# A new instruction order for a one-core linear-attention and feed-forward kernel, with other loads, buffers and step sizes

## The chip, the core and the metric

The kernel runs on one core of a Trainium2 chip. The core has a matrix engine (TensorE, PE in the profile), three engines for elementwise work (VectorE or DVE, ScalarE or ACT, GpSimd or POOL) and a queue engine (SyncE or SP). They run side by side, each its own instructions in the order of the program, and wait for one another by semaphores. DMA transfers are issued from POOL or from SP. The metric is the time of one execution on the device, in microseconds, median of several runs.

## The reference

Two stages follow each other. The first is a linear recurrence over 768 steps, for 4 batches and 8 heads of 48 channels, with a state of 48x48 for each head:

```python
for t in range(S):
    cur = np.einsum('bhd,bhe->bhde', u[None] * kt, vt)
    y[:, :, t] = np.einsum('bhd,bhde->bhe', rt, state + cur)
    state = wt[:, :, :, None] * state + np.einsum('bhd,bhe->bhde', kt, vt)
```

The second takes y as 3072 rows of 384 numbers (8 heads by 48) and computes

```python
a = x @ w1            # 384 -> 1024
b = x @ w2            # 384 -> 1024
h = a * b @ w3        # 1024 -> 1024
return h @ w_out      # 1024 -> 384
```

Inputs and output are float32.

## The kernel before

**Chunks and units.** The 768 steps are cut into 6 chunks of 128. A unit is one chunk of one or two batches: `UNITS` lists 13 of them, units 0 and 1 with one batch each, the others with two. A chunk's work is done with matrix products: the decay of a step inside the chunk is a cumulative sum of log(w), which `cs` (and, for some units, its transpose `csT`) gets from a product with a triangular matrix `LT`.

**Steps of a unit.** Each is a named step, recorded by `@op` and issued later. Loads: `win`, `kin`, `rin`, `vin`. ACT: `ln` (logarithm of w), then exponentials of the sums: `pc` (the chunk's decay), `ne`, and, by kind of unit, `iw` and `e`, or `et`. DVE: `KRk` and `KRr` (k and r scaled by decays), `rk`, `ruk`, `dg`, `dv` (the term with u). PE: `trk` and `trr` (transposes; `trke` and `trre` copy them out), `m` (the 128x128 products of r and k), `y` (with the state and with the masked `m`), `kv` (the new state's part), `yt` (transposes of y). DVE or ACT: `msk` (mask and copy `m`; or `mcp` on ACT and `maff` on DVE or POOL for the pairs in `POOL_MASK`), `T`, `S`, `Sb` (the state), `yb`, `xT`. In the sets `DMA_R`, `DMA_K` and `DMA_Y` a unit's transposes go by DMA from SP instead (`dtr`, `dtk`, `dty`). Units in `RAW` transpose r itself and multiply by `et`.

**Feed-forward.** w3 and w_out are multiplied first, into `w34` (`wt`: 4 transposes of 128x128 each, `w3Te` copies them out, `wm` 8 products, `w34e` copies out). Then for each unit, in pieces of 512 PSUM columns, `a` and `b` (6 products of 256 columns for a unit with two batches, 12 of 128 else), `asb` copies `a` out (ACT), `abT` multiplies the two (DVE). `o` is 8 products of 384 columns for 128 rows, `osb` copies out, `st` stores from SP.

**Order.** A long list, `ORDER`, names each step with its engine in the order in which it is issued; each engine runs its own steps of the list in that order. `BANKS` names the PSUM bank of each step. `warm` steps are products of zeros without a use of their own. Loads from POOL carry 8 semaphores in turn, so that the ninth waits until the first has landed.

**Lines.** In the profile L323 is any unit load, L350 a w3 load, L334 and L338 w1 and w2, L403 `ln`, L415 and L420 `cs`, L360 `wt`, L364 `w3Te`, L369 `wm`, L573 `m`, L592 `msk`, L608 and L614 `y`, L668 `kv`, L713 `a` and `b`, L724 `abT`, L730 `o`, L737 `osb`, L495, L510 and L642 the DMA transposes, L304 `warm`, L231 `table`. The step `table` asks for one set of ScalarE functions that holds both logarithm and exponential, and it is the first step on ACT.

Of the kernel before, what the change touches and what calls it, by code (L numbers as in the profile page):

```python
# [57 lines left out]
KRr_0@DVE m_1_0@PE mask@POOL KRk_0@DVE warm5@2 trk_0@PE rk_0@DVE kin_2@POOL msk_1_0@DVE trke_0@ACT warm5@2 m_0_0@PE
w3_2@POOL msk_0_0@DVE w1_0@POOL warm5@5 wm_1@PE w2_0@POOL wm_0@PE w1_1@POOL w3Te_3@ACT w34e_1@DVE y_0@PE w3Te_2@ACT
w34e_0@DVE y_1@PE win_3@POOL kv_0@PE kv_1@PE S_0@DVE wm_3@PE ln_2@ACT S_1@DVE Sb_1@DVE Sb_0@ACT w2_1@POOL csT_2@PE  # L60
w34e_3@ACT ruk_0@DVE vin_2@POOL wm_2@PE ruk_1@DVE et_2@ACT dg_0@DVE dg_1@DVE dv_0@DVE rin_3@POOL cs_2@PE w34e_2@DVE
trr_2@PE pc_2@ACT rk_2@DVE yd_0@PE ne_2@ACT dv_1@POOL KRr_2@DVE yb_0@ACT yt_0@PE yd_1@PE KRk_2@DVE w3_3@POOL wt_6_0@PE
wt_4_0@PE wt_7_0@PE xT_0@DVE wt_5_0@PE yb_1@DVE trk_2@PE ruk_2@DVE yt_1@PE kin_3@POOL a_0_0@PE trke_2@DVE xT_1@ACT
a_1_0@PE dg_2@DVE asb_0_0@ACT m_2_0@PE asb_1_0@ACT win_4@POOL msk_2_0@DVE b_0_0@PE b_1_0@PE abT_0_0@DVE m_2_1@PE
abT_1_0@DVE vin_3@POOL a_0_1@PE msk_2_1@DVE a_1_1@PE asb_0_1@ACT vin_6@POOL ln_3@ACT asb_1_1@ACT cs_3@PE ublk2@POOL
iw_3@ACT kin_5@POOL b_0_1@PE e_3@ACT b_1_1@PE pc_3@ACT ne_3@ACT abT_0_1@DVE kin_4@POOL abT_1_1@DVE kv_2@PE y_2@PE
S_2@DVE Sb_2@DVE rin_4@POOL rw_3@DVE KRr_3@DVE warm1@7 trr_3@PE trre_3@ACT win_5@POOL wt_4_1@PE wt_5_1@PE w3Te_4@ACT
wt_6_1@PE wt_7_1@PE w3Te_5@ACT vin_5@POOL wm_4@PE rk_3@DVE KRk_3@DVE ruk_3@DVE wm_5@PE rin_5@POOL ln_4@ACT w34e_4@DVE
w3Te_6@DVE iw_4@ACT dg_3@DVE cs_4@PE win_8@POOL w3Te_7@ACT wm_6@PE w34e_5@DVE e_4@ACT wm_7@PE vin_4@POOL pc_4@ACT
ne_4@ACT w34e_6@ACT dv_2@POOL kv_3@PE w34e_7@ACT trk_3@PE T_3@DVE o_1_0@PE trke_3@ACT S_3@POOL KRk_4@DVE win_6@POOL  # L70
yd_2@PE o_0_0@PE osb_1_0@DVE yb_2@DVE st_1_0@SP kin_6@POOL m_3_0@PE rk_4@DVE yt_2@PE osb_0_0@DVE rin_7@POOL m_3_1@PE
xT_2@ACT trk_4@PE ruk_4@DVE st_0_0@SP msk_3_1@DVE ln_5@ACT b_2_3@PE win_7@POOL trke_4@ACT a_2_1@PE rw_4@DVE rin_6@POOL
cs_5@PE msk_3_0@DVE iw_5@ACT a_2_2@PE asb_2_1@ACT dv_3@POOL a_2_0@PE e_5@ACT y_3@PE asb_2_2@ACT KRr_4@DVE kin_9@POOL
pc_5@ACT a_2_3@PE ne_5@ACT yb_3@DVE b_2_1@PE asb_2_0@ACT vin_8@POOL KRk_5@DVE trr_4@PE rw_5@DVE yt_3@PE trre_4@ACT
b_2_2@PE Sb_3@DVE xT_3@DVE vin_7@POOL b_2_0@PE KRr_5@DVE abT_2_2@DVE b_3_0@PE kin_7@POOL ln_6@ACT abT_2_0@DVE a_3_2@PE
abT_2_1@DVE asb_2_3@ACT m_4_1@PE a_3_0@PE dg_4@DVE iw_6@ACT win_10@POOL a_3_1@PE asb_3_0@ACT msk_4_1@DVE b_3_3@PE
dv_4@POOL asb_3_1@ACT b_3_2@PE abT_3_0@DVE m_4_0@PE abT_2_3@DVE win_9@POOL a_3_3@PE msk_4_0@DVE ln_7@ACT o_2_1@PE
kin_8@POOL asb_3_2@ACT rk_5@DVE asb_3_3@ACT abT_3_2@DVE y_4@PE iw_7@ACT kin_10@POOL abT_3_3@DVE b_3_1@PE osb_2_1@ACT
rw_7@DVE trr_5@PE st_2_1@SP rin_10@POOL ruk_5@DVE kv_5@PE trre_5@ACT yb_4@DVE kv_4@PE o_2_0@PE rin_8@POOL dg_5@DVE
T_4@DVE yt_4@PE dv_5@POOL osb_2_0@ACT trk_5@PE abT_3_1@DVE st_2_0@SP cs_6@PE xT_4@DVE trke_5@ACT o_3_0@PE rk_6@DVE  # L80
pc_6@ACT ne_6@ACT S_4@POOL T_5@DVE a_4_0@PE e_6@ACT ruk_6@DVE rin_9@POOL a_4_2@PE KRk_6@DVE Sb_4@ACT asb_4_0@ACT
dg_6@DVE a_4_3@PE kin_11@POOL osb_3_0@ACT b_4_1@PE ln_8@ACT rk_7@DVE st_3_0@SP rw_6@DVE win_11@POOL trk_6@PE
asb_4_2@ACT ruk_7@DVE a_4_1@PE iw_8@ACT KRr_6@DVE rin_11@POOL m_5_0@PE trke_6@ACT dv_6@DVE trr_6@PE b_4_0@PE
msk_5_0@DVE asb_4_1@ACT win_12@POOL o_3_1@PE trre_6@ACT abT_4_1@DVE m_6_0@PE abT_4_0@DVE osb_3_1@ACT b_4_2@PE
rin_12@POOL msk_6_0@DVE st_3_1@SP asb_4_3@ACT b_4_3@PE S_5@POOL m_5_1@PE abT_4_2@DVE cs_7@PE mcp_5_1@ACT vin_9@POOL
abT_4_3@DVE m_6_1@PE kv_6@PE dg_7@DVE e_7@ACT o_4_0@PE vin_10@POOL ne_7@ACT maff_5_1@DVE KRr_7@DVE pc_7@ACT
mcp_6_1@ACT y_5@PE KRk_7@DVE o_4_1@PE T_6@DVE osb_4_0@ACT dtr_7@SP vin_11@POOL Sb_5@ACT yb_5@DVE ln_9@ACT kv_7@PE
rk_9@DVE dtk_7@SP osb_4_1@ACT kin_12@POOL yt_5@PE rw_8@DVE iw_9@ACT cs_9@PE xT_5@DVE cs_8@PE st_4_1@SP e_9@ACT
rk_8@DVE b_5_3@PE st_4_0@SP maff_6_1@POOL ne_8@ACT a_5_3@PE pc_9@ACT pc_8@ACT e_8@ACT rw_9@DVE b_5_2@PE dv_7@POOL
T_7@DVE ne_9@ACT y_6@PE ln_10@ACT b_5_0@PE KRr_8@DVE ln_11@ACT a_5_1@PE S_7@POOL yb_6@DVE dtr_8@SP iw_10@ACT a_5_0@PE  # L90
vin_12@POOL ruk_8@DVE asb_5_1@ACT yt_6@PE ruk_9@DVE b_5_1@PE asb_5_0@ACT dg_8@DVE S_6@POOL xT_6@ACT a_5_2@PE
abT_5_0@DVE iw_11@ACT b_6_1@PE dv_8@DVE asb_5_2@ACT a_6_2@PE Sb_6@ACT abT_5_2@DVE b_6_2@PE asb_5_3@ACT abT_5_1@DVE
# [703 lines left out]
```

## Time and profile before

| what | before |
|---|---|
| median of 3 runs | 178.24 us (178.18 to 178.41) |
| span of the profiled execution | 176.7 us |
| around the span (median minus span) | 1.5 us |
| PE, DVE, ACT, POOL busy | 159.3, 131.3, 97.9, 92.8 us |
| mean granted clock of TensorE | 0.997 |
| moved by DMA | 25.70 MB |

The span runs from the first to the last instruction of the execution. A busy share counts an engine's instructions by their own durations; PE's are pipelined, so that its share overstates the work. An engine that is idle while another is full costs nothing; what counts is at which point PE, which carries the last step, was late and by whom.

### The profile page before, as it was taken

The page shows a single profiled execution, that of the slowest core. Times are in us where ns is not written, and L with a number is a line of the kernel's source. Part 1 is how long each engine was busy: PE and PEld are TensorE (multiplying, and loading weights), DVE is VectorE, ACT ScalarE, POOL GpSimd, SP SyncE. Part 2 cuts the span into 40 slices and gives each one's busy share as a digit, 9 for nine tenths or more (in the row PEclk, how much of TensorE's full clock was granted, in tenths as well). Part 3 has the DMA queues.
Part 4 walks back from the last instruction along what each step waited for, and adds up shares of the span by engine and source line. Part 5 has one row for each costly group of instructions (what it writes and reads, how often), then busy time and mean ns, then how long its engine had stood idle before and what let it go on. Part 6 is the DMA issues. An engine that isn't in the chain of part 4 may idle for free.

```text
span 176.7 us, 4637 instructions
## 1 busy us (share of the span) xinstructions
PE 159.3 (90%) x1935; PEld 118.0 (67%) x1935; DVE 131.3 (74%) x209; ACT 97.9 (55%) x160; POOL 92.8 (53%) x91
## 2 busy tenths in 40 slices
PE   2559898979799899999999889899999999999991
...
DVE  6012869857549999999999999987699957944420
...
DMA  5999999999999999999999997352745660151033
GB/s 95 171 164 192 190 195 211 221 177 192 139 169 186 226 192 147 190 170 177 223 193 143 190 120 142 100 125 67 147 108 121 132 153 1 26 156 45 4 113 111
DMA packets 104101, 25.70 MB, mean 145 GB/s; under 512 B 95216, under 2 KB 103024, under 8 KB 104080
## 3 DMA queue, kind: packets, MB, share of 16 engines
...
q14 instruction: 6, 0.05, 0.1%
...
## 4 chain that ended last, share of the span: by engine, by line
PE 67%; DVE 15%; DMA 6%; ACT 5%; issue 3%; SPq 0%; DVEq 0%
PE banks L713 30%; PE banks L730 13%; PE banks L369 6%; DMA win<-in_w_dram 5%; PE banks L573 4%; DVE rk L524 2%; DVE abT L724 2%; PE banks L614 2%; PE banks L415 2%; PE banks L360 2%; DVE rw L482 2%; PE banks L304 2%; DVE Mbf L592 2%; DMA xT<-yb 1%; DVE ruk L544 1%
## 5 line engine op out<-in xcount | busy, mean ns | idle before, releaser
L713 PE MATMUL banks<-xT,w_bf 128*128 128x256 bf16 (+1 forms) x624 | 69.0, 264 | 1.7 <-DVE abT L724 0.8
L713 PEld LDWEIGHTS <-w_bf 128*128 128x128 bf16 x624 | 55.6, 98 | 10.2 <-issue 2.0
L720 ACT COPY a_sb<-banks 128x512 f32<-128x512 f32 x48 | 28.0, 594 | 28.4 <-PE banks L713 20.0
L724 DVE TENSOR_TENSOR abT<-a_sb,banks 128x512 bf16<-128x512 f32 x48 | 31.4, 679 | 11.3 <-PE banks L713 9.1
L730 PE MATMUL banks<-w,abT 128*128 128x384 bf16 x192 | 34.3, 326 | 0.0
L730 PEld LDWEIGHTS <-abT 128*128 128x128 bf16 x192 | 18.2, 98 | 10.7
L592 DVE TENSOR_TENSOR Mbf<-banks,mask 128x1024 bf16<-128x1024 f32 x16 | 19.5, 1216 | 3.7 <-PE banks L573 3.7
L559 POOL TENSOR_TENSOR dv<-vin,dg 128x768 bf16<-128x768 bf16 (+1 forms) x10 | 14.9, 1497 | 8.6 <-issue 5.5
L323 POOL DMA_DIRECT2D vin<-in_v_dram x13 | 14.6, 1123 | 5.6 <-issue 3.9
L323 POOL DMA_DIRECT2D win<-in_w_dram x11 | 12.9, 1176 | 6.6 <-issue 4.1
L323 POOL DMA_DIRECT2D kin<-in_k_dram x13 | 14.6, 1126 | 1.7 <-DMA w_bf<-in_moe_w_dram 1.0
L737 ACT COPY osb<-banks 128x384 f32<-128x384 f32 x16 | 7.8, 486 | 13.8 <-PE banks L730 13.8
L323 POOL DMA_DIRECT2D rin<-in_r_dram x13 | 14.5, 1119 | 0.6 <-DMA vin<-in_v_dram 0.3
L304 PE MATMUL banks<-zeros 128*128 128x512 bf16 x29 | 9.8, 461 | 3.4 <-DVE zeros L235 3.4
L403 ACT ACTIVATE lw<-win 128x768 bf16<-128x768 f32 (+1 forms) x13 | 10.4, 811 | 4.5 <-DMA win<-in_w_dram 4.5
L369 PE MATMUL banks<-wo_bf,w3T 128*128 128x384 bf16 x64 | 11.2, 326 | 1.1 <-ACT w3T L364 1.1
L587 POOL TENSOR_SCALAR_AFFINE_SELECT Mbf<-Mbf 128x1024 bf16<-128x1024 bf16 x4 | 4.8, 1188 | 14.3 <-ACT Mbf L579 14.3
L550 DVE TENSOR_REDUCE dg<-ruk 128x16 f32<-128x768 bf16 (+1 forms) x13 | 11.4, 879 | 0.0
L573 PE MATMUL banks<-KRT 64*128 64x128 bf16 x192 | 9.6, 218 | 1.0 <-ACT Mbf L579 0.5
L415 PE MATMUL banks<-lw,LT 128*128 128x384 bf16 x24 | 6.4, 341 | 4.3 <-ACT lw L403 4.3
L364 ACT COPY w3T<-banks 128x1024 bf16<-128x1024 bf16 x6 | 6.0, 1016 | 7.3 <-PE banks L360 3.7
L633 DVE TENSOR_TENSOR yb<-banks,dv 128x768 bf16<-128x768 f32 x10 | 9.5, 952 | 0.7 <-PE banks L614 0.4
...
## 6 DMA issues: line engine op xcount, KB each, us to landing
...
```

The source lines that it names most:

```text
L304: nc.tensor.matmul(banks[:, at, :], lhsT=zeros[:, :C], rhs=zeros, start=True, stop=True)
L323: QUEUE[eng].dma_start(dst, src)
L369: nc.tensor.matmul(one(f"wm{fi}")[:, :DM], lhsT=w3T[fi % 2][:, gi, :], rhs=wo_bf[:, gi, :], start=(gi == 0), stop=(gi == FI - 1))
L403: nc.scalar.activation(LW[:, :, :D], ww, Act.Ln)
L550: nc.vector.reduce_sum(dgs, ruks, axis=AX.X)
L559: e.tensor_mul(dvs, vv, dgs[:, :, None].to_broadcast([C, bh, D]))
L573: nc.tensor.matmul(o[:, e, q, :], lhsT=KRTs[a:a + PAD, 0, b * HP + q, :], rhs=KRTs[a:a + PAD, 1, b * HP + q, :], start=True, stop=True)
L592: nc.vector.tensor_mul(Mbf[m], mview(), mask.rearrange("s (j q) t -> s j q t", j=2))
L713: nc.tensor.matmul(o[:, f, :], lhsT=wt[:, di, fi * P:(fi + 1) * P], rhs=x[:, di, :T], start=(di == 0), stop=(di == DI - 1))
L720: copier(eng)(sa, one(f"a{t}_{g}"))
L724: nc.vector.tensor_mul(ab[:, g * per:(g + 1) * per, :T], sa.rearrange("p (f t) -> p f t", t=T), one(f"b{t}_{g}").rearrange("p (f t) -> p f ...
L730: nc.tensor.matmul(one(f"o{t}_{b}")[:, :DM], lhsT=ab[:, fi, b * C:(b + 1) * C], rhs=w34[:, fi, :], start=(fi == 0), stop=(fi == FI - 1))
```

## The change

All 13 units compute the same as before. What changes:

- `ORDER` and `BANKS` are new as a whole. In the new order the transposes for `w34`, and `a` and `b`, come after more of the attention of units 0 to 3; `a` and `b` of units 0 to 3 are issued mixed; `o` comes later behind its `abT`.
- Buffers: `abT` has 8 instead of 3, `xT` 4 instead of 3. Buffers of `Mbf`, `a_sb` and `osb` are named in `BANKS` instead of taken in turn.
- Loads: r, k and v of unit 0 come by SP as float32 and are cast on chip (`rc` and `vc` on ACT, `kc` on DVE); u comes by SP as float32 and is cast by `uc` on DVE. w of units 0 and 1 came by SP before and still does. `ucol`, `ublk` and `ublk2`, whose result nothing read, are gone. w3's four loads are cut by rows (two blocks of 128 rows, all columns) instead of by quarters (four blocks, half of the columns).
- `y` is cut into `ys` (state) and `yi_0`, `yi_1` (one for each batch).
- Sets: `RAW` from {0, 1, 2} to {1, 2, 3, 6}; `N_PSUM` empty, so that `ne` writes SBUF as bfloat16 in all units; `DMA_K` from {7 to 12} to {5, 8 to 12}, `DMA_Y` from {7 to 12} to {4, 8 to 12}; `POOL_MASK` from eight pairs to (5,0), (9,0), (9,1); `Y_PE` from {0, 1, 2} to {0}.
- The step `table` stands between `xT_2` and `dv_3` instead of at the start. `S` may run on DVE.

```diff
-N_X = 3
+N_X = 4
-N_AB = 3
+N_AB = 8
+N_W3 = 4
-RAW = {0, 1, 2}
-N_PSUM = {0, 1, 2}
+RAW = {1, 2, 3, 6}
+N_PSUM = set()
-DMA_K = {7, 8, 9, 10, 11, 12}
-DMA_Y = {7, 8, 9, 10, 11, 12}
+DMA_K = {5, 8, 9, 10, 11, 12}
+DMA_Y = {4, 8, 9, 10, 11, 12}
-POOL_MASK = {(5, 1), (6, 1), (7, 1), (8, 1), (9, 1), (10, 1), (11, 1), (12, 1)}
-Y_PE = {0, 1, 2}
-F32_LOADS = set()
+F32_IN = {0}
+POOL_MASK = {(5, 0), (9, 0), (9, 1)}
+Y_PE = {0}
 ORDER = """
-win_1@SP table@ACT ones@DVE mask1@DVE win_0@SP w3_0@POOL ucol@SP w3_1@POOL padet@DVE padkr@DVE LT@POOL padlw@DVE
-kin_1@POOL zeros@DVE ln_1@ACT padr@DVE warm3@4 csT_1@PE rin_1@POOL cs_1@PE et_1@ACT rin_0@POOL pc_1@ACT ne_1@ACT
...
+zeros@DVE win_1@SP ones@DVE mask1@DVE win_0@SP win_2@POOL rin_0@SP padr@DVE kin_0@SP LT@POOL padlw@DVE rin_1@POOL
+vin_0@SP padkr@DVE padet@DVE u@SP ln_1@ACT kin_1@POOL warm0@1 cs_1@PE ln_0@ACT mask@POOL csT_1@PE iw_0@ACT cs_0@PE
+I128@POOL win_3@POOL rc_0@ACT w3_0@POOL rin_2@POOL kc_0@DVE rw_0@DVE ln_2@ACT kin_2@POOL pc_1@ACT warm3@9 csT_2@PE
+ne_1@ACT vc_0@ACT cs_2@PE rin_3@POOL et_1@ACT trw_1@PE pc_0@ACT pc_2@ACT ne_0@ACT vin_1@POOL KRk_1@DVE rk_0@DVE
...
+rin_5@POOL yb_2@DVE S_2@DVE yi_3_0@PE w2_1@POOL w34e_2@ACT yi_3_1@PE ln_4@ACT yt_2@PE w3_3@POOL wm_3@PE xT_2@DVE
+table@ACT dv_3@POOL w34e_1@DVE cs_4@PE w34e_3@ACT ln_5@ACT kv_3@PE w1_0@POOL yb_3@DVE pc_4@ACT wt_5_0@PE kin_5@POOL
...
+            if (x, t) in wide:
+                @op(f"{x}in_{t}")
+                def _(eng, x=x, src=src):
+                    QUEUE[eng].dma_start(wide[x, t], src)
+
+                @op(f"{x}c_{t}")
+                def _(eng, x=x, dst=dst):
+                    copier(eng)(dst, wide[x, t])
+                continue
...
-        f = slice(h // 2 * 4, h // 2 * 4 + 4)
-        gs = slice(h % 2 * 512, h % 2 * 512 + 512)
+        f = slice(h * FI // N_W3, (h + 1) * FI // N_W3)
...
-            nc.gpsimd.dma_start(w3_bf[:, f, gs], w3r[:, f, gs])
+            nc.gpsimd.dma_start(w3_bf[:, f, :], w3r[:, f, :])
...
-        @op(f"y_{t}")
+        if c:
+            @op(f"ys_{t}")
...
+        for b in range(nb):
+            @op(f"yi_{t}_{b}")
...
-                elif c < NC - 2:
-                    nc.gpsimd.tensor_mul(Sp, Tp, PCb)
                 else:
-                    nc.gpsimd.tensor_mul(Bp, Tp, PCb)
+                    e = nc.gpsimd if eng == "POOL" else nc.vector
+                    e.tensor_mul(Sp if c < NC - 2 else Bp, Tp, PCb)
```

More of the change, by code (lines that the diff above doesn't have):

```diff
@@ L58 @@
[L58 to L92, printed above, removed]
@@ new lines @@
+dg_0@DVE w3_1@POOL KRr_0@DVE trr_0@PE ln_3@ACT wo@POOL trre_0@DVE ne_2@ACT KRw_1@DVE warm1@3 m_0_0@PE m_1_0@PE
+msk_0_0@DVE kv_0@PE csT_3@PE vin_3@POOL wt_1_0@PE et_3@ACT msk_1_0@DVE wt_0_0@PE warm3@1 wt_0_1@PE vin_2@POOL trw_2@PE
+S_0@DVE yi_0_0@PE rk_1@DVE cs_3@PE ruk_1@DVE dv_0@POOL pc_3@ACT KRk_2@DVE win_4@POOL warm4@4 yd_0@PE dg_1@DVE
+ybc_0@ACT warm4@1 trw_3@PE w3Te_0@ACT rk_2@DVE win_5@POOL wt_1_1@PE KRw_2@DVE kv_1@PE trk_2@PE ne_3@ACT S_1@DVE
+yt_0@PE ruk_2@DVE w3_2@POOL w3Te_1@ACT warm3@1 yi_1_0@PE KRw_3@DVE dv_1@POOL trke_2@ACT kin_4@POOL yb_1@DVE Sb_0@ACT
@@ new lines @@
+m_2_1@PE KRk_3@DVE msk_2_1@DVE rin_4@POOL wt_3_0@PE m_2_0@PE dg_2@DVE wt_3_1@PE wt_2_0@PE wt_2_1@PE msk_2_0@DVE
+trk_3@PE yt_1@PE trke_3@ACT rk_3@DVE Sb_1@ACT ruk_3@DVE m_3_0@PE xT_1@ACT m_3_1@PE msk_3_0@DVE w1_1@POOL wm_0@PE
+msk_3_1@DVE wm_1@PE w34e_0@ACT w3Te_2@DVE dv_2@POOL w3Te_3@DVE yi_2_0@PE kv_2@PE dg_3@DVE yi_2_1@PE ys_3@PE wm_2@PE
+rin_5@POOL yb_2@DVE S_2@DVE yi_3_0@PE w2_1@POOL w34e_2@ACT yi_3_1@PE ln_4@ACT yt_2@PE w3_3@POOL wm_3@PE xT_2@DVE
+table@ACT dv_3@POOL w34e_1@DVE cs_4@PE w34e_3@ACT ln_5@ACT kv_3@PE w1_0@POOL yb_3@DVE pc_4@ACT wt_5_0@PE kin_5@POOL
@@ new lines @@
+ne_4@ACT T_3@DVE wt_4_0@PE wt_5_1@PE cs_5@PE iw_5@ACT w3Te_5@DVE wt_4_1@PE w2_0@POOL iw_4@ACT wm_5@PE w3Te_4@DVE
+KRk_4@DVE pc_5@ACT e_4@ACT rw_4@DVE vin_4@POOL trk_4@PE ne_5@ACT wm_4@PE KRr_4@DVE xT_0@ACT rk_4@DVE e_5@ACT trr_4@PE
+win_6@POOL trke_4@ACT a_0_1@PE trre_4@DVE yt_3@PE w34e_5@ACT a_2_3@PE rw_5@DVE vin_5@POOL KRr_5@DVE a_2_2@PE
+asb_2_3@ACT xT_3@DVE S_3@POOL a_1_1@PE asb_2_2@ACT a_3_2@PE asb_0_1@ACT ruk_4@DVE win_7@POOL w34e_4@ACT b_2_2@PE
+Sb_3@ACT trr_5@PE abT_2_2@DVE b_0_1@PE asb_3_2@ACT win_8@POOL m_4_1@PE abT_0_1@DVE wt_7_0@PE wt_6_0@PE Sb_2@DVE
@@ new lines @@
+b_1_1@PE asb_1_1@ACT msk_4_1@DVE wt_6_1@PE wt_7_1@PE w3Te_6@ACT b_3_2@PE kin_6@POOL abT_1_1@DVE a_1_0@PE dg_4@DVE
+w3Te_7@ACT ys_4@PE rin_7@POOL m_4_0@PE rk_5@DVE asb_1_0@ACT b_2_3@PE msk_4_0@DVE wm_6@PE abT_3_2@DVE ruk_5@DVE
+b_1_0@PE w34e_6@ACT KRk_5@DVE trre_5@ACT a_2_1@PE abT_1_0@DVE dv_4@POOL dtk_5@SP yi_4_0@PE abT_2_3@DVE asb_2_1@ACT
+a_3_1@PE b_0_0@PE rin_6@POOL ln_6@ACT yi_4_1@PE a_0_0@PE yb_4@DVE asb_3_1@ACT win_9@POOL b_2_1@PE asb_0_0@ACT
+dty_4_0@SP csT_6@PE abT_0_0@DVE kin_7@POOL b_3_1@PE et_6@ACT dg_5@DVE a_2_0@PE dty_4_1@SP rin_8@POOL abT_2_1@DVE
```

266 lines of the change are left out of this document (120 added, 146 removed).

## The prediction

> **What bounds the kernel now.** I read the page first (span, busy shares, slices), then the busy time by stage, the chain that ended last, ACT's timeline and the DMA issues by stretch.
>
> ```profile
> span 176.7 us, 4637 instructions
> PE 159.3 (90%) x1935; PEld 118.0 (67%) x1935; DVE 131.3 (74%) x209; ACT 97.9 (55%) x160; POOL 92.8 (53%) x91
> PE   2559898979799899999999889899999999999991
> DVE  6012869857549999999999999987699957944420
> DMA  5999999999999999999999997352745660151033
> ```
>
> PE is full from the eighth slice on, DVE from the 13th to the 25th, and DMA until about 107 us.
>
> ```profile
> 0.00:21.20 21.20, 13.40 (x105) 7.73 (x106) 7.90 (x24) 6.71 (x12) 16.71 (x24) 1.00 1.46 162
> 21.20:45.35 24.15, 20.89 (x310) 16.43 (x308) 18.00 (x33) 13.49 (x22) 15.79 (x16) 1.00 1.73 195
> 52.00:110.00 58.00, 55.88 (x718) 42.53 (x715) 57.32 (x80) 42.60 (x69) 43.60 (x38) 1.00 1.97 176
> 110.00:155.90 45.90, 45.36 (x609) 33.87 (x607) 38.84 (x61) 22.80 (x37) 11.43 (x9) 1.00 0.45 99
> ```
>
> (Stretch, its length, then PE, PEld, DVE, ACT, POOL busy, granted clock, DMA, GB/s.) From 52 to 110 us DVE idles 0.7 of 58 us, so PE and DVE share the bound there.
>
> ```profile
> 1.33 8.63 DMA win<-in_w_dram
> ...
> 45.35 2.77 PE banks L369 x16
> ...
> 78.73 2.62 PE banks L713 x24
> ...
> 155.89 10.65 PE banks L713 x96
> 166.55 6.51 PE banks L730 x40
> 173.08 0.48 ACT osb L737
> ```
>
> In the chain the reader sees the late w of unit 0 at the start, PE's pitch (24 products of `a` or `b` in 2.62 us, 40 of `o` in 6.51) and PE's end at 173.05, then 3.6 us for the last copy and store.
>
> **The measure.** I add up PE's useful work W, without `warm`, at the pitch of its steps: `a` or `b` 0.655 us (2.62/4), `o` and `wm` 1.30 (6.51/5), `m` 0.33, `y` 0.51 and 0.30 with state, `kv` 0.36, `cs` 0.53, `csT` and the transposes 0.45, `yt` 0.34, `wt` 0.22. Before, that is 96 x 0.655 + 32 x 1.30 + 24 x 0.33 + some 31 for the rest = 143.8 us. Time minus W is PE's lag: 16.7 at `wm_3` (24.7 us, W 7.9), 23.0 at `wm_5` (46.7 us, W 23.7), 27.4 at 110 us, 29.25 at the end. So 16.7 us go before PE has real work, 6.3 while `w34` and the attention of units 0 to 3 go on, 6.2 after. Span = W + final lag + 3.6; time = span + 1.54 (178.24 against 176.7).
>
> **The change, part by part.**
>
> PE's work: `yi`, `ys`, another `csT`, two `yd` less: W = 143.95. The steps of `y`, cut in three, have the same products.
>
> DVE: five more `msk` at 1.216 (+6.1), three fewer `maff` (-2.1), `S`, `dv`, `osb`, `w3Te`, `trre` to it (+1.1, +1.4, +1.1, +1.4, +1.1), fewer `w34e`, `rw`, `Sb` (-3.8): by durations +6.3; start to start (an instruction overlaps the next by 0.06 us) 137.6 against 131.7 us. POOL loses seven arithmetic instructions (6.3 us by their rows) and four issues.
>
> Loads: w3's first two pieces are no longer ahead of unit 0's w. In the trace win_1, alone, took 2.8 us to land; win_0, behind it on SP but beside 2 MB of w3 on POOL's queue, landed at 9.97. The 96-KB loads after them landed 0.7 us apart. Beside the 192-byte rows of win_2 I put win_0 at 5.0 (bounds: 4.3, at that spacing, and 9.97 as now). r, k, v of unit 0 and u follow on SP at one such spacing each, doubled for sharing: 6.4 to 11, before their casts at about 7, 8.5, 11 and 13.6. SP has nothing else to do until a transpose at 55 us.
>
> ACT's tables: the listing of the built programs shows one table load on ACT before and eight in the changed kernel, since `table` no longer comes first and each change between `ln` and an exponential loads a set; the eighth is `table` itself, and none follow.
>
> ```profile
> 0.80 1.28 ACT L231 ACT_TABLE_LOAD   x1 [0.80 <-PEq L780]
> 3.60 0.52 ACT L403 ACTIVATE lw<-win 128x384 bf16<-128x384 f32 x1 [1.51 <-DMA win<-in_w_dram]
> ```
>
> One costs 1.28 us, here hidden behind win_1's landing; the first stays hidden. Five (ahead of `iw_0`, `ln_2`, `pc_1`, `ln_3`, `ne_2`) stand in an ACT queue that is full: from `ln_0`'s end at 5.5 us to `trke_2` there are 22 more instructions (`iw_0` 0.48, two casts of 0.49, `ln` 0.85 twice, `ne` 0.48 twice and 0.82 twice, `et` 0.60, 1.02, 1.02, `pc` four times 0.18, `trke` 0.59 and 1.03, `e_0` 0.48, `ybc_0` 0.49, `w3Te` 1.01 twice), 13.7 us, less 1.3 of overlap, plus 6.4: `trke_2` ends at 24.3. `m_2_1` follows with W 7.9, lag 16.4: what the earlier w wins (some 5 us) the tables take.
>
> The Trainium skill ("ScalarE: Activation LUTs", What ACT_TABLE_LOAD costs) gives 1283 ns for the load and about 1380 ns for a drain besides, 2.66 us for each switch. The trace agrees on the load; on the drain it shows nothing, as ACT waited for w then. By the page those five would cost 13.3 us instead of 6.4; the rival below prices a dearer switch from the row.
>
> From `m_2_1` DVE leads: `msk` four times, `dg_2`, `rk_3`, `ruk_3`, `w3Te_2`, 7.5 us, to 32.1; then `wm_2`; three more on DVE and `yt_2`, `wm_3` to 36.1. ACT, idle until `wm_2` ends at 33.4, has `w34e_2`, a load, `ln_4`, a load, `w34e_3`, `ln_5` (38.5), then eight exponentials and copies of 4.6 us in all to `xT_0`: 43.1. PE meanwhile does `cs_5`, `wm_5`, `trk_4`, `wm_4`, `trr_4`. So `a_0_1` starts at 43.2, and with some ten handovers of 0.07 (the chain's small pieces of issue) 43.9: W 23.7, lag 20.2 against 23.0 before. Bounds: 19.5 (no handover) and 25 (win_0 as late as now).
>
> Weights land later: w1 and w2 stand behind eight more unit loads, which landed 1.5 us apart, so w2_0 comes at 50 to 52 instead of 31.6; it is needed by `b_1_0` at W 34.9, 55 us. w1_1, 39 to 41, is needed at 43.9. On POOL, `dv_2` waits behind w1_1's issue, which waits for wo's landing (27); `yb_2` needs it at 33: hidden. If these covers go, PE waits by the same amount.
>
> After 43.9 us: DVE has done 30.5 us of its work by `KRr_4` at 42.4, so it lags 11.9 us behind its own sum. In the new order DVE's sum is ahead of PE's by 4.5 to 7.4 us at all points up to `yi_10_0` (before: 1 to 2.7). PE cannot lag less than 11.9 + 7.4 = 19.3 there: again both are full. `abT` in eight buffers lets `o` fill PE where DVE is late. For what PE loses from here the trace gives 6.2 as the upper end (the same W, before) and 1.8 as the lower (from 110 us on, where DVE has room); I take 4.8, nearer the upper, since both engines are full for longer. Final lag 25.0.
>
> Transposes of units 4 and 5 go by DMA while loads fill the queues:
>
> ```profile
> KRT<-KR SPq DMA_TRANSPOSE x4, 7.2
> ...
> KRT<-KR SPq DMA_TRANSPOSE x8, 3.1
> ```
>
> (The issues of 86 to 108 us and those of 108 to 160: us to landing.) `dtk_5`, issued at about 54.5, lands at 62 and `m_5_1` is due at 61.6; `dty_4`'s second lands at 67.4 for `a_4_2` at 66.5. Between -0.5 (PE and ACT freed of `trk` and `yt`) and +3; I take 0.5, within the 4.8. The last stores stay as they are: the tail is 3.6.
>
> Sum: 143.95 + 25.0 + 3.6 + 1.54 = 174.1, or 174 us; ends 143.95 + 19.5 + 1.8 + 5.1 = 170.4 and 143.95 + 25 + 6.2 + 5.1 = 180.3.
>
> **The rivals.**
>
> *Dearer table switches* (slower). If a load also empties ACT's pipeline ahead and fills it behind, a switch may cost up to twice its row. Seven lie on the path (five before `trke_2`, two before `xT_0`): 7 x 1.28 = 9.0 us more, lag 29.2 at `a_0_1`; the rest then has room, 1.8: 31.0, time 180.1. It decides from 0.6 us a switch (4.2 us of lag). Against it: the listing has no instruction around the loads. 13%.
>
> *PE and DVE in each other's way* (slower). DVE has 1.2 us more to do after `a_0_1` than before, and its two-input operations can stand behind POOL's (`rk_8` took 2.67 us for 0.55). If each handover goes wrong as often as now and DMA transposes and loads come 2 to 4 us late besides, the loss is 9 instead of 4.8: 178.4; it decides from 8.8. 22%.
>
> *Nothing lost later*: attention is far ahead, loads are in time, and only 1.8 is lost: 171.1. 13%.
>
> *No change*: gains and tables cancel, 178 within 0.2% (about what this kernel's runs can tell apart). 5%.
>
> **Chances.** The forecast (171.5 to 177.5) has 47%, the better case 13%: faster 0.60, same 0.05, slower 0.35. The range, 170.0 to 181.0, leaves out about a tenth at each end; the forecast's own is 171.5 to 177.5.
>
> **What would show it.** Right: eight table loads of 1.28 us, six in the first 21 us; win_0 landed by 5.5; `m_2_1` at 24 to 25; `a_0_1` at 43 to 45; DVE over 95% busy from 50 to 130 us; the last `o` done at 169. Wrong: gaps over 1.5 us between a table load and the activation behind it, `win_0` still after 8 us, PE waiting for w1, w2 or `dtk_5`, or a DVE idle by more than 6 us between 45 and 130 while PE is late.

## The result, and the profile after

| what | before | after |
|---|---|---|
| median, runs beside each other | 178.21 us | 190.31 us (188.02 to 191.4, 4 runs) |
| ratio to before | | 1.0615, 95% interval 1.0543 to 1.0688 |
| profiled execution | | 191.22 us, span 189.5 us |
| mean granted clock of TensorE in it | 0.997 | 0.928 |

The forecast was 174.0 us with a range of 170 to 181; the kernel is 6% slower. Medians are of all runs, ratios only of those within 1.5% of a kernel's fastest, a limit that the profiled execution here exceeds. The first experiment takes a second trace, of an execution of 190.36 us with a clock of 0.954.

In the changed kernel a few lines have other numbers: L401 is `ln`, L471 `iw`, L425 `pc`, L432 `ne`, L456 `et`, L323 the casts of unit 0, L548 `m`, L646 `kv`, L593 `yi`, L687 `a` and `b`, L703 `o`, L662 `S`, L536 `dv`, L328 the unit loads from POOL, L301 `warm`.

The page after: span, busy times, and the rows of 40 slices (4.74 us each) for PE, DVE, TensorE's clock and DMA.

```profile
span 189.5 us, 4629 instructions
PE 163.7 (86%) x1939; PEld 124.1 (65%) x1939; DVE 136.0 (72%) x215; ACT 98.7 (52%) x161; POOL 83.0 (44%) x80
PE   2947796898799990999998899998899799989992
DVE  5025747976776972649999997999998888462361
PEclk9975579589999997599999999999999999999999
DMA  6999999999999899994099999729697934124015
```

The reader sees three things that the page before does not have: TensorE at half clock in three places (in slices 3 to 6, 8 to 9 and 16 to 17), one slice (the 16th, 71 to 76 us) in which PE is all but empty, and DMA empty around the 20th (90 us) while much is still to be loaded. DVE is full only from the 19th slice (85 us), not from the 13th.

Busy time by stretch of the changed kernel (stretch, its length, then PE, PEld, DVE, ACT, POOL busy with their instructions, granted clock, DMA share, GB/s):

```profile
0.00:24.30 24.30, 15.62 (x108) 8.88 (x109) 10.54 (x33) 17.26 (x24) 19.90 (x25) 0.75 1.52 174
24.30:44.00 19.70, 17.26 (x231) 12.79 (x230) 14.70 (x21) 6.98 (x13) 9.62 (x9) 0.79 1.72 189
52.00:110.00 58.00, 52.25 (x703) 42.63 (x701) 45.88 (x70) 37.18 (x63) 31.72 (x28) 0.94 1.72 128
110.00:150.00 40.00, 37.46 (x478) 28.54 (x477) 37.89 (x56) 18.00 (x31) 13.74 (x11) 1.00 1.12 140
```

DVE idles 12.1 of the 58 us from 52 to 110; before it was 0.7. The bound that the forecast counted on, PE and DVE both full, is not reached there.

The chain that ended last: its shares, the pieces that are new in it, and PE's end (start, length, what):

```profile
PE 49%; DMA 18%; DVE 14%; ACT 10%; issue 4%; SPq 2%; DVEq 0%; ACTq 0%
```

```profile
1.94 6.55 DMA wide_r<-in_r_dram
...
66.20 9.44 DMA KRT<-KR
...
125.41 7.77 DMA vin<-in_v_dram
...
143.79 5.39 DMA xT<-yb
...
182.14 3.92 PE banks L703 x24
```

A load of unit 0, a transpose of unit 5, a load of unit 10 and a transpose of unit 9 now stand on the path. In the forecast's own measure, PE's lag (time less useful work W done until then):

| step | W | forecast | after | the kernel of the ninth experiment |
|---|---|---|---|---|
| `m_2_1` | 7.9 | 16.4 (at 24.3 us) | 23.6 (31.5 us) | 16.6 (24.5 us) |
| `a_0_1` | 23.7 | 20.2 (43.9 us) | 30.0 (53.7 us) | 20.2 (43.9 us) |
| `m_5_1` | 41.1 | | 34.6 (75.7 us) | 22.6 (63.7 us) |
| `kv_10` | 93.3 | | 39.9 (133.2 us) | 23.5 (116.8 us) |
| end of PE | 143.95 | 25.0 | 42.1 | 25.6 |

W plus the last lag plus a tail of 3.5 to 3.6 is the span in each column. (The ninth kernel has 0.8 us more of products than this W from `m_5_1` on, which its lags include.) So 7.2 us are lost before `m_2_1` more than forecast, 2.6 more up to `a_0_1`, and 7.3 more from there to the end (12.1 against 4.8), 17.1 in all.

### The profile page after: what moved, and what is told of

It is laid out like the page before. It is cut to its first block, busy times and chain, and to the rows that moved or that the text cites. A ratio compares the mean times of both kernels' runs of the same rounds, so it can differ in the third digit from the quotient of the medians.

```text
span 189.5 us, 4629 instructions
## 1 busy us (share of the span) xinstructions
PE 163.7 (86%) x1939; PEld 124.1 (65%) x1939; DVE 136.0 (72%) x215; ACT 98.7 (52%) x161; POOL 83.0 (44%) x80
## 4 chain that ended last, share of the span: by engine, by line
PE 49%; DMA 18%; DVE 14%; ACT 10%; issue 4%; SPq 2%; DVEq 0%; ACTq 0%
PE banks L687 18%; PE banks L703 11%; DMA xT<-yb 6%; DMA KRT<-KR 5%; PE banks L373 4%; DMA vin<-in_v_dram 4%; DMA wide_r<-in_r_dram 3%; DVE abT L697 3%; PE banks L548 3%; DVE Mbf L567 2%; PE banks L364 2%; PE banks L593 2%; DVE KR L437 2%; PE banks L301 2%; DVE yb L611 1%
## 5 line engine op out<-in xcount | busy, mean ns | idle before, releaser
L687 PE MATMUL banks<-xT,w_bf 128*128 128x256 bf16 (+1 forms) x624 | 70.7, 266 | 2.1 <-DMA xT<-yb 2.1
L687 PEld LDWEIGHTS <-w_bf 128*128 128x128 bf16 x624 | 55.5, 98 | 9.9 <-DMA xT<-yb 1.9
L692 ACT COPY a_sb<-banks 128x512 f32<-128x512 f32 x48 | 27.6, 589 | 41.7 <-PE banks L687 37.3
L703 PE MATMUL banks<-w,abT 128*128 128x384 bf16 x192 | 34.5, 326 | 0.2 <-DVE Mbf L567 0.2
L536 POOL TENSOR_TENSOR dv<-vin,dg 128x768 bf16<-128x768 bf16 (+1 forms) x9 | 12.6, 1405 | 38.8 <-DVE dg L527 34.8
L567 DVE TENSOR_TENSOR Mbf<-banks,mask 128x1024 bf16<-128x1024 f32 x21 | 25.2, 1217 | 3.7 <-PE banks L548 3.5
L703 PEld LDWEIGHTS <-abT 128*128 128x128 bf16 x192 | 18.2, 98 | 11.0 <-issue 0.4
L548 PE MATMUL banks<-KRT 64*128 64x128 bf16 x192 | 9.8, 240 | 7.4 <-DMA KRT<-KR 4.3
L328 POOL DMA_DIRECT2D win<-in_w_dram x11 | 13.0, 1184 | 4.7 <-ACT lw L401 1.9
L328 POOL DMA_DIRECT2D vin<-in_v_dram x12 | 13.8, 1156 | 1.8 <-DMA w_bf<-in_moe_w_dram 1.6
L328 POOL DMA_DIRECT2D rin<-in_r_dram x12 | 13.9, 1162 | 0.0
L328 POOL DMA_DIRECT2D kin<-in_k_dram x12 | 13.9, 1158 | 0.0
L611 DVE TENSOR_TENSOR yb<-banks,dv 128x768 bf16<-128x768 f32 (+1 forms) x12 | 11.0, 918 | 3.8 <-PE banks L593 3.7
L548 PEld LDWEIGHTS <-KRT 64*128 64x128 bf16 x192 | 6.7, 105 | 10.1 <-DMA KRT<-KR 4.6
L373 PE MATMUL banks<-wo_bf,w3T 128*128 128x384 bf16 x64 | 12.9, 353 | 0.0
L437 DVE TENSOR_TENSOR KR<-kin,NEt 128x768 bf16<-128x768 bf16 (+1 forms) x13 | 9.3, 718 | 4.0 <-ACT NEt L432 4.0
L708 ACT COPY osb<-banks 128x384 f32<-128x384 f32 x14 | 6.4, 482 | 10.9 <-PE banks L703 8.4
L301 PE MATMUL banks<-zeros 128*128 128x512 bf16 x25 | 10.5, 544 | 1.3 <-DVE zeros L242 1.3
L401 ACT ACTIVATE lw<-win 128x768 bf16<-128x768 f32 (+1 forms) x13 | 10.3, 796 | 2.2 <-DMA win<-in_w_dram 2.2
L432 ACT ACTIVATE NEt<-banks 128x768 bf16<-128x768 f32 (+1 forms) x13 | 10.0, 771 | 2.7 <-DVE KR L437 2.7
## 6 DMA issues: line engine op xcount, KB each, us to landing
rin<-in_r_dram POOLq DMA_DIRECT2D x11, 192.0 KB, 10.2
kin<-in_k_dram POOLq DMA_DIRECT2D x11, 192.0 KB, 10.2
```

The source lines that it names most:

```text
L301: nc.tensor.matmul(banks[:, at, :], lhsT=zeros[:, :C], rhs=zeros, start=True, stop=True)
L328: QUEUE[eng].dma_start(dst, src)
L373: nc.tensor.matmul(one(f"wm{fi}")[:, :DM], lhsT=w3T[fi % 2][:, gi, :], rhs=wo_bf[:, gi, :], start=(gi == 0), stop=(gi == FI - 1))
L437: nc.vector.tensor_mul(KRs[:, 0, :, :D].rearrange("t (b h) d -> t b h d", b=nb), kk.rearrange("t (b h) d -> t b h d", b=nb), n)
L536: e.tensor_mul(dvs, vv, dgs[:, :, None].to_broadcast([C, bh, D]))
L548: nc.tensor.matmul(o[:, e, q, :], lhsT=KRTs[a:a + PAD, 0, b * HP + q, :], rhs=KRTs[a:a + PAD, 1, b * HP + q, :], start=True, stop=True)
```

## The experiments

My theory after the result had four parts: (1) the seven table loads more on ACT delay the start; (2) `dtk_5` and `dty_4` land late among the loads and leave PE idle; (3) `S_5` and `dv_9` on POOL, waiting for DVE, hold back the loads behind them; (4) TensorE's clock falls behind each idle stretch and makes it dearer. The rivals: the order itself (DVE and PE in each other's way) costs the time, whatever stands at these places; and, for the tables, a dearer switch than the row shows. The kernel before took 177.45 to 177.52 us beside these runs.

**1. The changed kernel once more**, without an edit.

> The changed kernel as it is, beside the others on the same chip. Both theories expect 188 to 191 us. A second trace tells which delays come back: the eight table loads of 1.28 us, the wait of m_5_1 for the transpose of unit 5 (4.3 us of idle PE), the half clock of TensorE at 12 to 25, 32 to 39 and 73 to 80 us. A delay that does not come back is no part of the cause.

190.52 us (189.62 to 191.44), ratio 1.073 (1.068 to 1.079). PE around `m_5_1` in this trace (start, length, what, idle time before and its releaser), and the stretches around it:

```profile
67.09 1.47 PE L687 MATMUL banks<-xT,w_bf 128*128 128x256 bf16 x12
73.57 1.03 PE L548 MATMUL banks<-KRT 64*128 64x128 bf16 x16 [5.01 <-DMA KRT<-KR]
```

```profile
61.00:69.00 8.00, 7.56 (x100) 6.44 (x97) 6.59 (x11) 5.14 (x8) 8.00 (x8) 1.00 1.68 115
69.00:73.00 4.00, 0.00 (x0) 0.00 (x0) 0.60 (x2) 0.18 (x1) 2.14 (x2) 0.92 2.18 104
73.00:80.00 7.00, 6.43 (x81) 4.38 (x82) 3.19 (x4) 2.63 (x4) 2.32 (x2) 0.56 2.53 136
80.00:88.00 8.00, 8.00 (x117) 7.15 (x113) 6.37 (x12) 5.90 (x10) 0.00 (x0) 1.00 1.08 131
```

`dtk_5`, issued at 63.4, lands 10.1 us later; PE stands still for 5.0 us; then the clock is 0.56 for 7 us and `m` takes 1.03 us for 16 products. The table loads, this wait and the half clock behind it come back as they were. Of the half clock ahead of 40 us only half comes back: 10.2 us in three pieces instead of 20.5. `a_0_1` therefore starts at 50.9 instead of 53.7 us, but the span ends only 0.8 us earlier, so that most of these 2.8 us are given back later.

**2. One table load instead of eight**: `table` second in the order.

```diff
-zeros@DVE win_1@SP ones@DVE mask1@DVE
+zeros@DVE win_1@SP table@ACT ones@DVE mask1@DVE
...
-wm_3@PE xT_2@DVE table@ACT dv_3@POOL
+wm_3@PE xT_2@DVE dv_3@POOL
```

> The changed kernel with the step table as the first on ACT, as before; nothing else is moved. One table load instead of eight. Theory 1 (the table loads hold up the start): ACT has 9.0 us less to do before xT_0, a_0_1 starts 6 to 9 us earlier (at 45 to 48 us instead of 53.7), and as PE then waits less the clock drops of the first 40 us shrink; the time falls by 6 to 9 us, to 180 to 183 us. Theory 2 (the start is held by the loads of unit 0, above all r, which landed at 8.5 us, and by DMA): ACT waits for them instead, and the time falls by less than 3 us.

Inconclusive as a time: 189.91, 187.65, 181.44 and one run of 263.07 us whose mean clock was 0.571. The trace says why it need not show: PE is 3.5 us less late at `b_3_2` (24.1 against 27.6), but `m_5_1` comes at 73.38, as before, since `dtk_5` now takes 13.5 us (59.88 to 73.33). In this execution, of 189.91 us, one late transfer swallowed what the other edit won. The run of 181.44 us lies within the 180 to 183 of the first theory; it has no trace, so that what differed in it stays open.

**3. PE kept busy ahead of `m_5_1`**: 19 products of zeros in the gap.

```diff
-rin_8@POOL abT_2_1@DVE m_5_1@PE
+rin_8@POOL abT_2_1@DVE warm2@19 m_5_1@PE
```

> The changed kernel with 19 products of zeros (some 4 us at full clock) ahead of m_5_1, in the time in which PE waits for the DMA transpose of unit 5's k. They do not shorten the wait. If the half clock at 73 to 80 us follows from this idle stretch, it is gone, and the time falls by 1.5 to 2.5 us. If the clock drops for another reason, the record still shows 0.5 there and the time stays within 1 us.

186.48 us (185.33 to 188.39), ratio 1.0485 (1.0427 to 1.0542), 4.0 us less than the changed kernel, though PE has more to do. The gap is filled and the clock stays:

```profile
71.62 4.05 PE L301 MATMUL banks<-zeros 128*128 128x512 bf16 x18
76.09 0.62 PE L548 MATMUL banks<-KRT 64*128 64x128 bf16 x16 [0.42 <-DMA KRT<-KR]
```

```profile
69.00:73.00 4.00, 3.95 (x36) 2.97 (x35) 3.29 (x5) 2.20 (x3) 4.00 (x5) 1.00 1.18 124
73.00:80.00 7.00, 6.58 (x93) 4.02 (x92) 2.76 (x4) 2.63 (x4) 3.39 (x3) 1.00 2.65 126
```

The same 16 products take 0.62 us instead of 1.03, while `dtk_5` is as late as it was (9.6 us). From `m_5_1` to `a_4_2` PE takes 4.8 us here and 7.2 in run 1. So part 4 holds: behind the idle stretch of 5 us the clock alone cost PE 2.4 us, as expected. The rest of the 4.0 isn't shown to be the clock: the profiled execution of this kernel is the slowest of its four (188.39 us), its start is 3 us later than in run 1, and what it gains on run 1 at the end arises behind `kv_10`.

**4. The kernel before with `table` late**: seven table loads, nothing else of the change.

```diff
-win_1@SP table@ACT ones@DVE
+win_1@SP ones@DVE
...
-ln_3@ACT asb_1_1@ACT
+table@ACT ln_3@ACT asb_1_1@ACT
```

> The kernel before with the step table moved behind the exponentials of unit 2 (just ahead of ln_3), so that ACT makes seven table loads instead of one; nothing else is changed. Theory 1: the price of a load is 1.28 us where ACT is full and nothing where it waits. In this order ACT waits for w at the start (1.5 and 3.0 us idle), so that two or three of the six further loads are hidden; the others delay et_0, ne_0 and unit 2: 2 to 5 us slower, 180 to 183 us. If a switch costs a drain of as much again: 5 to 9 us, 183 to 187 us. If the loads are hidden in this order: within 1 us.

181.93 us (181.73 to 182.56), ratio 1.0256 (1.0215 to 1.0297): 4.5 us for six loads more, with a clock of 0.999. ACT in that trace:

```profile
6.97 1.28 ACT L403 ACT_TABLE_LOAD   x1
8.84 0.52 ACT L403 ACTIVATE lw<-win 128x384 bf16<-128x384 f32 x1 [0.59 <-DMA win<-in_w_dram]
9.38 1.28 ACT L427 ACT_TABLE_LOAD   x1
10.68 0.17 ACT L427 ACTIVATE pc<-banks 128x4 f32<-128x4 f32 x1
...
25.05 1.28 ACT L403 ACT_TABLE_LOAD   x1
26.35 0.84 ACT L403 ACTIVATE lw<-win 128x768 bf16<-128x768 f32 x1
```

The activation behind a load starts 0.01 to 0.02 us after it unless a transfer is late (8.84). Six loads at 1.28 are 7.7 us, so that 3.2 of these don't show in the time: the price is the row's, the rival's is not seen.

**5. The transposes of KR of unit 5 and y of unit 4 on PE** (the rest as changed, eight table loads).

```diff
-DMA_K = {5, 8, 9, 10, 11, 12}
-DMA_Y = {4, 8, 9, 10, 11, 12}
+DMA_K = {8, 9, 10, 11, 12}
+DMA_Y = {8, 9, 10, 11, 12}
...
-abT_1_0@DVE dv_4@POOL dtk_5@SP yi_4_0@PE
+abT_1_0@DVE dv_4@POOL trk_5@PE trke_5@ACT yi_4_0@PE
...
-dty_4_0@SP csT_6@PE abT_0_0@DVE kin_7@POOL b_3_1@PE et_6@ACT dg_5@DVE a_2_0@PE dty_4_1@SP
+csT_6@PE abT_0_0@DVE kin_7@POOL b_3_1@PE yt_4@PE et_6@ACT xT_4@ACT dg_5@DVE a_2_0@PE
```

> The changed kernel with the transposes of unit 5's k and unit 4's y back on PE (trk_5, trke_5 on ACT, yt_4, xT_4 on ACT, in banks that are free then) instead of by DMA; eight table loads as in the changed kernel. Theory 1 (m_5_1 waits for a DMA transpose that lands late because the loads fill the queues): the idle stretch of 4 to 5 us ahead of m_5_1 goes, with it the half clock of 7 to 10 us behind it; PE and ACT have 0.8 and 1.8 us more to do. 5 to 7 us faster than the changed kernel: 183 to 186 us. Theory 2 (PE would wait there anyway, for loads or for DVE): under 2 us.

184.21 us (182.45 to 186.37), ratio 1.0355 (1.0289 to 1.0422): 6.3 us less than the changed kernel. PE's wait at `m_5_1` is gone, and the clock is full from 34.7 us on:

```profile
69.84 0.62 PE L548 MATMUL banks<-KRT 64*128 64x128 bf16 x16 [0.23 <-ACT xT L634]
```

The rival, by which PE would have lost the time elsewhere, falls here.

**6. Both**: the edits of 2 and 5 together.

> Both: table first, and the transposes of units 4 and 5 on PE. With the table alone the start was 3.5 us earlier and all of it was lost at m_5_1, which stayed at 73.5 us. Theory 1: with the late transpose gone the 3.5 us stay: 3 to 5 us faster than with the transposes alone, 178 to 181 us. If the loads are what holds the middle, the two together give no more than the transposes alone.

179.78 us over ten runs (177.23 to 181.05), ratio 1.0063 (1.0011 to 1.0116; of six of the ten). The table's edit, masked in 2, is worth 4.4 us now by the medians, within the 3 to 5 expected. What is left is seen on POOL and at `kv_10` (first three lines POOL, last PE):

```profile
69.61 1.16 POOL L328 DMA_DIRECT2D win<-in_w_dram  x1 [0.29 <-issue]
79.48 1.00 POOL L662 TENSOR_TENSOR Sst<-Tst,pc 128x384 f32<-128x384 f32 x1 [8.72 <-DVE Tst L654]
...
113.20 1.21 POOL L328 DMA_DIRECT2D vin<-in_v_dram  x1
...
121.00 0.43 PE L646 MATMUL banks<-vin,KR 128*64 128x48 bf16 x16 [1.45 <-DMA vin<-in_v_dram]
```

POOL waits 8.7 us for DVE ahead of `S_5`, with nine loads of units 8 to 12 behind it; `vin_10`, behind `dv_9`, is issued at 113.2 and lands at 121.

**7. Six of those loads earlier**: as 6, and `kin_9`, `rin_10`, `vin_8` ahead of `S_5`, `vin_10`, `rin_12`, `vin_11` right behind `S_7`.

```diff
-abT_4_0@DVE S_5@POOL a_5_3@PE
+abT_4_0@DVE kin_9@POOL rin_10@POOL vin_8@POOL S_5@POOL a_5_3@PE
...
-S_7@POOL m_7_1@PE
+S_7@POOL vin_10@POOL rin_12@POOL vin_11@POOL m_7_1@PE
```

> As the run with both, and on POOL three loads (k of unit 9, r of unit 10, v of unit 8) moved ahead of S_5 and three (v of 10, r of 12, v of 11) ahead of dv_9, so that they no longer stand behind a product that waits for DVE. Theory 3 (POOL's in-order queue starves the DMA and v of unit 10 lands late for kv_10): the DMA's idle stretch of some 8 us near 88 us goes, kv_10 no longer waits for DMA, 1 to 2.5 us faster than the run with both. If these loads are not on the path: within 0.5 us.

175.15 us (174.91 to 177.99), ratio 0.9869 (0.983 to 0.9908). POOL and PE at the same places:

```profile
74.15 1.14 POOL L328 DMA_DIRECT2D vin<-in_v_dram  x1 [0.36 <-PE banks L509]
78.47 1.00 POOL L662 TENSOR_TENSOR Sst<-Tst,pc 128x384 f32<-128x384 f32 x1 [3.18 <-DVE Tst L654]
...
92.66 1.21 POOL L328 DMA_DIRECT2D vin<-in_v_dram  x1
...
117.32 0.43 PE L646 MATMUL banks<-vin,KR 128*64 128x48 bf16 x16
```

No wait at `kv_10`; PE's lag grows by 0.9 us from `a_4_2` to `kv_10`, not by 3.6 as in 6. The medians differ by 4.6 us, the two profiled executions by 2.2 (177.38 and 175.22). Of these 2.2, 1.4 stand already at `a_0_1` (46.2 against 44.8 us), ahead of the first moved load: the kernel of 6 had half clock from 14.3 to 21.2 us, this one had none. So 4.6 us overstates what the loads alone are worth; expected were 1 to 2.5. The kernel now beats the one before, by 1.3%.

**8. The start's casts behind unit 1's work**: as 6, and `vc_0` on ACT behind `e_0`, `uc`, `ruk_0`, `dg_0` on DVE behind `KRw_1`, so that late v and u of unit 0 hold nothing else.

```diff
-ne_1@ACT vc_0@ACT cs_2@PE
+ne_1@ACT cs_2@PE
...
-kin_3@POOL uc@DVE trke_1@ACT warm7@1 trk_0@PE ruk_0@DVE e_0@ACT trke_0@DVE et_2@ACT dg_0@DVE w3_1@POOL
+kin_3@POOL trke_1@ACT warm7@1 trk_0@PE e_0@ACT vc_0@ACT trke_0@DVE et_2@ACT w3_1@POOL
...
-KRw_1@DVE warm1@3 m_0_0@PE
+KRw_1@DVE uc@DVE ruk_0@DVE dg_0@DVE warm1@3 m_0_0@PE
```

> As the run with both, and the steps at the start that wait for SP's float32 loads moved back: vc_0 on ACT behind e_0, and uc, ruk_0, dg_0 on DVE behind KRw_1. Theory 4 (casts that wait in an in-order queue for v and u, landed at 11.4 and 14 us, hold up the start): m_0_0 starts 1.5 to 2.5 us earlier, and the time falls by 1 to 2 us against the run with both. If the clock or the loads of units 2 and 3 hold the start, the time stays within 0.5 us.

176.69 us over ten runs (175.94 to 177.27), ratio 0.9958 (0.9936 to 0.998): `m_2_1` at 24.4 instead of 28.1 us. Of these 3.7 us the profiled execution has 1.5 left at `a_0_1` and 1.2 at its end; the medians differ by 3.1, where 1 to 2 were expected.

**9 to 11. All of it, and all but one thing.** The ninth kernel has the edits of 6, 7 and 8; the tenth is the ninth with `table` where the change put it (eight loads); the eleventh is the ninth with the DMA transposes of units 4 and 5.

> The changed kernel with everything that the runs so far pointed at: one table load, the transposes of units 4 and 5 on PE, six loads of units 8 to 12 ahead of POOL's waiting steps, and vc_0, uc, ruk_0 and dg_0 behind the work of unit 1. Theory (the places add up: the start gives about 2 to 3 us and POOL's loads 3 to 5 us against 179.8): 172 to 174.5 us, final lag 22 to 25, kv_10 without a step. Rival (PE and DVE bound what is left, so that time won at the start is given back later, as both engines are full): 174.5 to 176, the final lag that of the run with POOL's loads alone, about 26, however early the start is.

> As the kernel with everything, only the step named table stands where the changed kernel has it, so ACT loads eight tables. Theory (each load costs its 1.28 us where ACT is full, five before unit 2's transposes and two before xT_0, some of it hidden, as the 4.5 us for six loads in the kernel before): 4 to 8 us above the kernel with everything, the first a product 4 to 7 us later, and TensorE at half clock for longer before 40 us. Rival (the loads are hidden behind the late r, k and v of unit 0, and only the late transposes kept the changed kernel back): within 2 us of it.

> As the kernel with everything, only KR of unit 5 and y of unit 4 are transposed by DMA, as in the changed kernel. Theory (the transposes land 9 to 14 us after their issue among the loads, PE idles for 4 to 5 us ahead of m_5_1 and then runs at half clock for 7 us): 5 to 9 us above the kernel with everything, the step of the lag at m_5_1 4 to 8 us. Rival (PE's idling there is slack that the loads on POOL's queue later take anyway, so it is made up with these out of the way): within 2 us of it, the lag at 110 us the same in both.

| kernel | median us | ratio to before (interval) |
|---|---|---|
| 9, all edits | 174.87 (174.43 to 175.57) | 0.9858 (0.9792 to 0.9923) |
| 10, eight table loads | 181.84 (181.18 to 184.24) | 1.0233 (1.0163 to 1.0304) |
| 11, DMA transposes | 180.03 (179.26 to 180.62) | 1.0141 (1.008 to 1.0202) |

So 7.0 us (6.4 by the runs that the ratios take) hang on the tables and 5.2 on the two transposes, both within what the theory gave; the start's casts, with POOL's loads out of the way, are worth 0.3 us (175.15 to 174.87), as the rival of run 9 said: what is won at the start is mostly given back. By the medians from 190.5 to 174.9, transposes 6.3, tables 4.4, POOL's loads 4.6 and casts 0.3 make up the whole difference. With the casts first (8, then 9) they have 3.1 and POOL's loads 1.8, so that only the sum of these two, 4.9, doesn't depend on the order. The new order itself, with these four things changed, is 1.4% faster than the old one (0.8 to 2.1%).

The start of the ninth and of the tenth kernel (stretches as above):

```profile
11.00:24.00 13.00, 9.56 (x136) 6.73 (x136) 11.33 (x23) 8.72 (x14) 11.36 (x13) 1.00 1.88 182
24.00:36.00 12.00, 9.53 (x154) 6.68 (x155) 10.74 (x14) 3.37 (x8) 6.03 (x6) 1.00 1.54 201
```

```profile
11.00:24.00 13.00, 7.68 (x81) 5.45 (x84) 8.09 (x18) 10.21 (x16) 10.19 (x11) 0.82 1.87 181
24.00:36.00 12.00, 9.41 (x123) 7.47 (x124) 7.49 (x12) 5.64 (x10) 5.63 (x6) 0.78 1.52 199
```

With the loads, PE is handed its work later, has 13 us with 7.7 busy, and its clock falls to 0.82 and 0.78; without them it stays at 1.00. `m_2_1` comes at 31.7 instead of 24.5 us, 7.2 us for five loads of 1.28.

In the eleventh kernel the size fits the theory but the mechanism only in part (lines around `m_5_1` and `a_4_2`):

```profile
65.39 0.62 PE L548 MATMUL banks<-KRT 64*128 64x128 bf16 x16 [2.61 <-DMA KRT<-KR]
...
72.51 1.69 PE L687 MATMUL banks<-xT,w_bf 128*128 128x256 bf16 x14 [2.18 <-DMA xT<-yb]
```

PE waits 2.6 us for `dtk_5` (7.7 us to landing) and 2.2 for `dty_4`, and the clock stays full there. PE is 1.2 us later already at `a_0_1`, through half clock at 26 to 33 us that this edit doesn't touch, 4.1 at `a_4_2` and 6.0 at the end, where it waits twice more for transposes of y (0.6 and 1.0 us). So about 3 of the 5.2 us are the two transposes' own, and why the later ones come late in this kernel was not tried.

## Why the prediction was wrong, step by step

**Right.** Eight table loads of 1.28 us; win_0 landed at 4.8 us (forecast 5.0); PE's useful work and the tail. Once the four delays are taken out, the loss from `a_0_1` on is near the forecast too: 5.4 us in the ninth kernel, 0.8 of it products, against the 4.8 taken. Its time, 174.87 against 174.0, is near by luck as well (below), and DVE is busy 53.2 of 58 us from 52 to 110 there, not over 95%. (One reading of the page before was a little off: PE's ninth and 11th slices are at 7 tenths, not full. No term hangs on it.)

**The price of a table load: right.** ACT of the changed kernel at the start:

```profile
5.33 1.28 ACT L471 ACT_TABLE_LOAD   x1
6.62 0.52 ACT L471 ACTIVATE iw<-lw 128x384 bf16<-128x384 bf16 x1
8.51 0.51 ACT L323 CAST rin<-wide_r 128x384 bf16<-128x384 f32 x1 [1.36 <-DMA wide_r<-in_r_dram]
9.04 1.28 ACT L401 ACT_TABLE_LOAD   x1
10.34 0.84 ACT L401 ACTIVATE lw<-win 128x768 bf16<-128x768 f32 x1
...
13.80 0.51 ACT L323 CAST vin<-wide_v 128x384 bf16<-128x384 f32 x1 [0.76 <-DMA wide_v<-in_v_dram]
...
23.22 1.02 ACT L456 ACTIVATE ETt<-banks 128x1024 bf16<-128x1024 f32 x1 [1.10 <-PE banks L450]
26.49 0.18 ACT L425 ACTIVATE pc<-banks 128x8 f32<-128x8 f32 x1 [2.24 <-DVE KRT L467]
27.54 0.48 ACT L608 CAST yb<-banks 128x384 bf16<-128x384 f32 x1 [0.87 <-PE banks L602]
```

Behind each load the next activation starts within 0.02 us. The Trainium skill ("ScalarE: Activation LUTs", What ACT_TABLE_LOAD costs) adds about 1380 ns of drain to each switch; these rows and the 4.5 us for six loads in experiment 4 don't show it. The rival of dearer switches, which ended on the right side with 180.1 us, and whose lag of 29.2 at `a_0_1` is near the 30.0 measured, had the wrong mechanism.

**Wrong: "stand in an ACT queue that is full".** From `ln_0`'s end at 5.3 us to `trke_2` ACT was to be busy all the time: 13.7 us of instructions, less 1.3, plus 6.4 of loads. It was not: it waits 1.36 (r of unit 0), 0.76 (v), 0.63, 1.10, 2.24 and 0.87 us, 7.0 in all, and `trke_2` ends at 31.5 instead of 24.3. In the ninth kernel, without the loads, ACT still waits 6.9 us there. The queue is one side of a chain that goes to and fro between DMA, ACT, PE and DVE; the sum of one engine's durations was only its lower bound, and the loads, being links of that chain, add in full (7.2 us for five, experiment 10, with the clock that falls behind them). That `m_2_1` of the ninth kernel falls on my figure (24.5) is two errors of 6 to 7 us that cancel there: no table loads, and the waits.

**Wrong: the landings.** "r, k, v of unit 0 and u follow on SP at one such spacing each, doubled for sharing: 6.4 to 11" measured 8.5, 10.1, 13.8 and 15.6 us. These casts stand ahead of unit 1's work in in-order queues. Moved away, they gave 3.1 us in one setting and 0.3 in another, by the medians.

**Missing: TensorE's clock.** I assumed 1.0 throughout. In the changed kernel it was 0.5 at 12.0 to 25.6, 32.4 to 39.3 and 73.4 to 80.2 us, each time behind a stretch in which PE had had little to do; `wm_0` alone took 2.59 us where a run at full clock has 1.46. The repetition, with half as much half clock ahead of 40 us, reaches `m_2_1` 0.9 and `a_0_1` 2.8 us earlier, so that 1.9 of the 2.6 us more between them can be put down to it. The Trainium skill ("TensorE: Matmul & The Clock Gate", What's actually happening) says that the clock is halved after an idle window of some 3.4 us and restored after a busy one of that length. The traces agree on the length, since the three stretches last 13.7, 6.8 and 6.8 us, and on the third, which comes behind 4.3 us without products. They don't bear out that the window has to be idle. Of the 3.41 us ahead of the first two stretches PE was busy 1.42 and 1.81 (the first numbers behind the length):

```profile
8.55:11.96 3.41, 1.42 (x13) 0.76 (x12) 0.63 (x2) 3.36 (x4) 3.41 (x4) 1.00 1.46 212
29.03:32.44 3.41, 1.81 (x35) 1.17 (x32) 2.57 (x6) 2.68 (x4) 0.74 (x1) 1.00 1.78 213
```

Its longest gaps there were 2.0 and 1.5 us. In the eleventh kernel 1.64 us of work in 3.41 (to 26.4 us) were followed by half clock, 1.69 in 3.40 (to 74.2 us) were not, so what decides isn't worked out here.

**Mis-sized: `dtk_5`.** "Between -0.5 and +3; I take 0.5". It was issued at 66.2, only 5.2 us before PE was ready for it (the forecast had 7.1), took 9.4 us instead of the 7.2 of the row, and PE idled 4.3 (5.0 in the repetition), with half clock behind it: 6.3 us by experiment 5, together with the transposes of unit 4. Why it took longer than its row isn't shown: DMA's share was 1.77 from 66.2 to 75.7 us and 1.90 in the stretch of the row, 86 to 108 us before.

**Not seen: POOL's queue.** I named `dv_2` behind w1_1 as hidden, and it was. I did not ask what stands behind `S_5` and `dv_9`, which wait for DVE: loads for units 8 to 12. With DVE late, POOL stood for 8.7 us (experiment 6) to 12.3 us (experiment 1) while DMA ran empty, `vin_10` was issued too late and PE lost 2.7 us up to `kv_10` (3.6 against 0.9, experiments 6 and 7).

**The rivals.** "DMA transposes and loads come 2 to 4 us late besides" was the nearest in its mechanism, at 178.4 us (its terms add up to 178.3) and 22%; it had the right kind of mishap, but as one term of 4 us instead of two with a clock behind them. The late start, which makes 9.8 of the 17.1 us, stood in none as waits between the engines. The range's upper end, 180.3, took in a win_0 as late as before, and nothing for ACT's waits.
